# An attention and token-MLP kernel: a table of scheduler rules by stretches of 16 score tiles, filled where it was empty

## The chip, the cores and the metric

The kernel runs on one core of a Trainium2 chip. The metric is the device time of one execution in microseconds, as the median of several runs. The engines have these names in the profile: PE is TensorE (matmuls; PEld its weight loads), ACT is ScalarE, DVE is VectorE, POOL is GpSimd, SP is SyncE, which issues the DMAs.

## What is computed

The input x has 2048 rows of 640. It is normalised by row, goes once through an attention block with 32 heads of 20 columns, and once through an MLP that mixes along the rows (the "token MLP"); the result is x plus their product.

```python
xn = _layernorm(x, axis=-1)
qkv = (xn @ wqkv).reshape(B, S, 3, H, Dh).transpose(2, 0, 3, 1, 4)   # H = 32, Dh = 20, S = 2048
scores = jnp.einsum("bhqd,bhkd->bhqk", q, k) * (Dh ** -0.5)
p = _softmax(scores, axis=-1)
o = jnp.einsum("bhqk,bhkd->bhqd", p, v)
s = o.transpose(0, 2, 1, 3).reshape(B, S, D) @ wo
...
h = _layernorm(xn, axis=-1)
u = _gelu(jnp.einsum("bsd,sf->bdf", h, w1) + b1)                      # w1: 2048 x 1536
y = jnp.einsum("bdf,fs->bds", u, w2) + b2                             # w2: 1536 x 2048
g = _silu(y.transpose(0, 2, 1))
return x + s * g
```

## The kernel before

**Tiling.** The scores are computed transposed, in tiles of 128 keys by 512 queries of one head. With 32 heads, 16 key blocks and 4 query blocks there are 2048 tiles. Heads are taken in 8 groups of four; a group and a query block make a pass of 64 tiles (32 such lots in all, the last one in two halves). Three tiles of different heads run side by side on TensorE (L1279), since a head's keys fill only 32 of its rows. Of the 8 banks of PSUM, two groups of three hold score tiles, one (bank 6) collects the output of a pass, and one (bank 7) is shared by all other work and by single tiles.

**Two ways to an exponential.** Most tiles go to ScalarE, which takes the exponential of two or three banks in one instruction (`emit_exp`, L1308) into a ring of 20 buffers `pt_sb`. The rest go to VectorE in units of four tiles, one per head of the group, with one key block: VectorE turns a score into the bits of a bf16 number by an addition and a maximum (`emit_op1`, L1319), makes three shifted copies of the four tiles at once (`emit_top`, L1357), and TensorE adds the four versions with scaled copies of V (`vs_sb`), which averages out the error of that exponential. A ScalarE tile costs one PV matmul, a VectorE tile four. Both kinds of PV run in `emit_pv` (recorded at L1376, four heads side by side). At most five key blocks of a pass can go to VectorE. At the end of a pass VectorE transposes bank 6 and divides by the row sums (`ep_steps`, L1500 to L1518).

**Everything else** is cut into jobs with requirements and a due time: layer norms, the projections of q, k and v (recorded at L648 and L691), the token MLP (`mlp_steps`, L648 too, as all matmuls in column parts are recorded there; in row parts, beside score tiles, at L656), its activations (tanh on ScalarE at L844 and L849, products on VectorE), the output projection (L965), its product with g (L980, L994, in the tail L1714 and L1730), and the residual add (L1006). Due times are counted in passes: the number of score tiles started, divided by 64.

**The order of the work** is found while the program is built: `schedule()` keeps a clock for each engine with fixed costs for each operation, asks each engine for its candidates, and emits the one that can start first. The emitted order is fixed for the chip. TensorE's candidates come from `pe_cands` (L1772). Its rules are class constants:

- SLACK (0): by how many ns other TensorE work may overrun the time at which the next score tiles must start so that ScalarE doesn't wait (`lim + self.SLACK`).
- MINJ (640): of a job that needs a change of matmul kind, at most this much of its remaining run of matmuls must fit before that time (`jfit`, L1893).
- ROOM (3): with fewer free `pt_sb` buffers than this, PV goes first.
- LATE (1.0) and JOBF (4): a job overdue by more than LATE passes, or JOBF or more free buffers, put jobs ahead of PV.
- PARTS ((2,)): in which parts the PV of a VectorE unit may be taken before its copies are all done.
- LEND (1800): the third bank of a group is lent to a VectorE tile if VectorE has less than this many ns of such work before it (`do_st`, L1995).
- DON (True): whether new VectorE units may be started (`d_claimable`, L1200).
- TOPP (38), EVP (36): VectorE's precedence of the shifted copies and of evictions of PSUM, lower first (`eng_cands`, L2049).

If no candidate fits and TensorE would pause, it may emit filler matmuls (`emit_fill`, L1393).

**The table.** Before each step of the main loop, the scheduler looks whether another 16 score tiles have been started; if so it sets the constants from row `win` of PLAN, where a digit is an index into the list of that option in OPTS. PLAN is empty, so the class constants hold throughout.

```python
    def tune(self, w):
        if w < len(self.PLAN):
            for (name, vals), i in zip(self.OPTS, self.PLAN[w]):
                setattr(self, name, vals[int(i)])
...
            if nclaim[0] >= win * self.WIN:
                self.tune(win)
                win += 1
```

Of the kernel before, what the change touches and what calls it, by code (L numbers as in the profile page):

```python
# [265 lines left out]
class _Kern:  # L266
# [19 lines left out]
    SLACK, MINJ = 0.0, 640.0  # L286
# [13 lines left out]
    JOBF = 4  # L300
# [4 lines left out]
    LATE = 1.0  # L305
# [10 lines left out]
    TOPP, EVP = 38.0, 36.0  # L316
    GROT = 1
    OPTS = (
        ("SLACK", (120.0, 40.0, 200.0, 320.0)),
        ("MINJ", (640.0, 320.0, 1000.0)),  # L320
        ("ROOM", (3, 6, 0)),
        ("DRIDE", (400.0, 150.0, 700.0)),
        ("LEND", (1800.0, 1300.0, 2400.0, 700.0, 0.0)),
        ("PARTS", ((2,), (2, 1), (3, 1), (1,), ())),
        ("LATE", (2.0, -9.0, 99.0)),
        ("DON", (True, False)),
        ("LONE", (False, True)),
        ("CONFL", (True, False)),
        ("TOPP", (38.0, 22.0)),
        ("EVP", (24.0, 36.0)),  # L330
        ("FGAP", (40.0, 150.0)),
        ("GROT", (1, 0)),
    )
    PLAN = ()
    PARTS = (2,)
    DX = (1, 2, 3)
    V1A, V1B = 1.2, 3.0
# [68 lines left out]
# [4 lines that stand above are left out]
# [1770 lines left out]
```

## Time and profile before

| | us |
|---|---|
| median of 3 runs | 756.44 (756.05 to 757.03) |
| the profiled execution | 757.3 |
| its span | 755.5 |
| ScalarE busy | 730.5 (97%) |
| VectorE busy | 720.5 (95%) |
| TensorE busy | 709.7 (94%) |
| GpSimd busy | 15.5 (2%) |
| granted TensorE clock | 1.000 |

The span runs from the first to the last instruction of the profiled execution; the 1.8 us between it and the execution's time lie around it. Busy times are shares of the span. In a row of the page's groups, the line, engine, operation and tiles are followed by the count, then the busy time in us and the mean ns of one instruction, then the engine's idle time just before such instructions and what ended most of it. In the timeline and in the chain, the first number is the start in us and the second the length.

### The profile page before, as it was taken

The numbers are of one execution on the slowest core, as the hardware profiler recorded it, in microseconds if no ns is written. First come the engines' busy times: TensorE is split into PE (matmuls) and PEld (weight loads), VectorE is DVE, ScalarE is ACT, GpSimd is POOL, SyncE is SP. The second block draws the span as 40 slices with busy tenths as digits, with TensorE's granted clock in tenths as the row PEclk, the third lists the DMA queues.
The fourth block names the chain that finished last, engine by engine and source line by source line (L and its number), as shares of the span: only waits on it lengthen the run. The fifth ranks groups of instructions, "written<-read, shape, count | busy, mean of one in ns | idle before, by whom it ended". The sixth has DMA issues, their size and how long they took to land.

```text
span 755.5 us, 23583 instructions
## 1 busy us (share of the span) xinstructions
PE 709.7 (94%) x10508; PEld 242.5 (32%) x10520; DVE 720.5 (95%) x1321; ACT 730.5 (97%) x708; POOL 15.5 (2%) x23
## 2 busy tenths in 40 slices
PE   8889999999999999999999998999999999999997
PEld 7332222232233323332232232323233332332333
DVE  8899989999998999999999999999999999999997
ACT  5899999999999999999999999999999999999994
POOL 4200000000000000000000000000000000000000
PEclk9999999999999999999999999999999999999999
DMA  9745211110121301312011104122225510041012
GB/s 234 146 113 63 63 22 37 20 37 5 40 60 20 76 6 45 85 34 46 13 31 27 30 7 119 19 51 50 60 80 88 130 39 30 2 152 47 26 35 71
DMA packets 119738, 42.66 MB, mean 56 GB/s; under 512 B 79172, under 2 KB 118468, under 8 KB 119588
## 3 DMA queue, kind: packets, MB, share of 16 engines
q1 hardware_dynamic: 119636, 41.15, 23.6%
q8 instruction: 82, 1.34, 0.8%
q14 instruction: 20, 0.16, 0.1%
HBM read 26.37 MB, written 10.22 MB: 48 GB/s over the span
## 4 chain that ended last, share of the span: by engine, by line
ACT 84%; PE 11%; DVE 3%; DMA 1%; SPq 0%; issue 0%
ACT pt_sb L1308 82%; PE ps_all L648 4%; PE ps_all L1279 4%; PE ps_all L1376 3%; ACT zt_sb L849 1%; ACT zt_sb L844 1%; DMA regA<-in_A_x_dram 1%; DVE regC L568 1%; DMA xnT_sb<-regC 0%; PE ps_all L965 0%; PE ps_all L633 0%; DVE bst_sb L530 0%; DVE bst_sb L532 0%; DVE dt_sb L1319 0%; DVE v_sb L1114 0%
## 5 line engine op out<-in xcount | busy, mean ns | idle before, releaser
L1308 ACT ACTIVATE pt_sb<-ps_all 128x1024 bf16<-128x1024 f32 (+2 forms) x683 | 711.7, 1220 | 6.1 <-PE ps_all L1279 3.8
L1319 DVE TENSOR_SCALAR dt_sb<-ps_all 128x512 uint16<-128x512 f32 x496 | 327.7, 679 | 18.8 <-PE ps_all L1279 9.7
L1279 PE MATMUL ps_all<-qk_sb 32*128 32x512 bf16 (+1 forms) x2128 | 268.6, 376 | 32.5 <-ACT pt_sb L1308 28.9
L1357 DVE TENSOR_SCALAR dt_sb<-dt_sb 128x2048 uint16<-128x2048 uint16 x372 | 239.2, 683 | 1.6
L1279 PEld LDWEIGHTS ps_all<-qk_sb 32*128 32x128 bf16 x2128 | 68.3, 91 | 289.5 <-ACT pt_sb L1308 243.8
L1376 PE MATMUL ps_all<-pt_sb,v_sb 128*21 128x512 bf16 (+1 forms) x1616 | 127.0, 374 | 2.3 <-DVE v_sb L1114 1.0
L1376 PE MATMUL ps_all<-dt_sb,vs_sb 128*21 128x512 bf16 (+1 forms) x1536 | 124.1, 375 | 0.1
L648 PE MATMUL ps_all<-regB,regA 128*32 128x128 bf16 (+1 forms) x1492 | 63.6, 299 | 0.0
L648 PE MATMUL ps_all<-regC,regA 128*32 128x128 bf16 (+1 forms) x1448 | 62.5, 296 | 0.1
L1376 PE MATMUL ps_all<-dt_sb,v_sb 128*21 128x512 bf16 (+1 forms) x512 | 49.0, 378 | 0.3 <-issue 0.3
L1376 PEld LDWEIGHTS ps_all<-pt_sb,v_sb 128*21 128x21 bf16 x1616 | 32.9, 91 | 50.9 <-issue 32.5
L648 PE MATMUL ps_all<-xnT_sb,wqk_sb 128*32 128x512 bf16 x640 | 45.6, 382 | 0.2 <-DVE qs_sb L1117 0.2
L1376 PEld LDWEIGHTS ps_all<-dt_sb,vs_sb 128*21 128x21 bf16 x1536 | 30.0, 91 | 33.1 <-issue 22.9
L648 PEld LDWEIGHTS ps_all<-regB,regA 128*32 128x32 bf16 x1492 | 26.9, 96 | 25.2 <-issue 12.9
L648 PEld LDWEIGHTS ps_all<-regC,regA 128*32 128x32 bf16 x1448 | 26.2, 96 | 24.9 <-issue 14.0
L656 PE MATMUL ps_all<-regC,regA 32*128 32x512 bf16 x88 | 33.9, 385 | 0.0
L965 PE MATMUL ps_all<-wv_sb,xnT_sb 128*128 128x128 bf16 (+1 forms) x150 | 25.4, 296 | 1.9 <-issue 1.1
L1500 DVE STREAM_TRANSPOSE tr_sb<-ps_all 128x512 f32<-128x512 f32 x31 | 21.9, 706 | 0.0
L648 PE MATMUL ps_all<-wv_sb,xnT_sb 128*32 128x480 bf16 x320 | 21.1, 369 | 0.0
L1376 PEld LDWEIGHTS ps_all<-dt_sb,v_sb 128*21 128x21 bf16 x512 | 12.5, 90 | 24.3 <-issue 21.0
L648 PEld LDWEIGHTS ps_all<-xnT_sb,wqk_sb 128*32 128x32 bf16 x640 | 13.2, 95 | 18.4 <-issue 8.1
L823 DVE TENSOR_SCALAR zt_sb<-ps_all,b2h_sb 128x512 bf16<-128x512 f32 (+1 forms) x32 | 17.2, 540 | 0.6 <-PE ps_all L648 0.6
(88 smaller groups left out, 347.5 us busy)
## 6 DMA issues: line engine op xcount, KB each, us to landing
regA<-in_B_w_dram SPq DMA_DIRECT2D x6, 1024.0 KB
regA<-in_B_w_dram SPq DMA_DIRECT2D x8, 768.0 KB
qk_sb<-qk_scratch_dram SPq DMA_DIRECT2D x56, 80.0 KB
qk_scratch_dram<-qs_sb SPq DMA_DIRECT2D x32, 128.0 KB
regA<-in_A_x_dram SPq DMA_DIRECT2D x6, 640.0 KB
ok_scratch_dram<-on_sb SPq DMA_DIRECT2D x96, 20.0 KB
out_dram<-regC SPq DMA_DIRECT2D x3, 640.0 KB
wqk_sb<-in_A_wqkv_dram SPq DMA_DIRECT2D x2, 480.0 KB
```

Of the source, the lines that this page charges most:

```text
L568: steps.append(("dve", lambda e, b=b: e.tensor_scalar(regC[:, b, :], regC[:, b, :], st_sb[:, 6, b:b + 1], None, ALU.mult), [S_("r2"), S_(f ...
L648: fns.append(lambda e, c=c, e_=e_: e.matmul(oc(c, e_), lhsT[:, c:e_], rhs, start=start, stop=stop, tile_position=(0, c)))
L656: row = lambda g: (lambda e: e.matmul(oc(0, 128), lhsT[32 * g:32 * g + 32, :], rhs[32 * g:32 * g + 32, :], start=False, stop=False, tile_p ...
L823: steps.append(("dve", lambda e, z=z, i=i, jj=jj: e.tensor_scalar(z[:, c0:c0 + n], ps(bk, n, i * n), 0.5, bias[:, jj:jj + 1], ALU.mult, AL ...
L844: steps.append(("act", lambda e: e.activation(tt_, tt_, AF.Tanh, scale=1.5957691216), [stt], [stt], f"th{j}", ac(n)))
L965: steps.append(("pe", lambda e, c=c: e.matmul(ap, oT_sb[:, c, b * 128:(b + 1) * 128], wo_ap[:, c, c0:c0 + n], start=(opens and c == 0), st ...
L1279: pr.pe(lambda e, outp=outp, lhsT=lhsT, rhs=rhs, g=g: e.matmul(outp, lhsT, rhs, start=True, stop=True, tile_position=(32 * g, 0)), reads=q ...
L1308: tk = pr.act(lambda e: e.activation(outp, inp, AF.Exp, scale=math.log(2.0) / 128.0), reads=[bank_slot[b] for b in banks[:n]], writes=[S_( ...
L1319: tk = pr.dve(lambda e: e.tensor_scalar(w, src, WOFF, 0.0, ALU.add, ALU.max), reads=[bank_slot[bk]], writes=[S_(f"dt{d['tl'][0]}_{g}")], n ...
L1357: tk = pr.dve(lambda e: e.tensor_scalar(dst, src, dk, None, ALU.add), reads=[S_(f"dt{b}_{g}") for b in inb for g in range(4)], writes=[S_( ...
L1376: pr.pe(lambda e: e.matmul(outp, lhsT, rhs, start=(k == 0), stop=last, tile_position=(0, 32 * g)), reads=reads, writes=[bank_slot[AB]], na ...
L1500: steps.append(("dve", lambda e: e.transpose(tr_sb[:, :], ps(AB)), [bank_slot[AB]], [S_("tr")], f"epT{q}", 632.0))
```

## The change

PLAN gets 128 rows of 15 digits, one for each stretch of 16 score tiles. OPTS is extended so that index 0 of each list is the value of the class constant: SLACK 0.0 and LATE 1.0 are put in front, EVP is turned round, and JOBF is added. Rows of zeros restate the constants. Twenty rows hold another digit: SLACK 120 in stretch 14; LEND 2400 in 17 and in 117 to 119; TOPP 22 in 44; PARTS (1,) in 45; ROOM 6 in 58 and 59; MINJ 1000 in 82 to 89 and in 118; MINJ 320 in 91; LATE 99 with DON False in 101; LEND 1300 in 126. A row holds for its stretch and is replaced by the next one. Work, tiles and buffers are as they were.

```diff
     OPTS = (
-        ("SLACK", (120.0, 40.0, 200.0, 320.0)),
+        ("SLACK", (0.0, 120.0, 40.0, 200.0, 320.0)),
         ("MINJ", (640.0, 320.0, 1000.0)),
         ("ROOM", (3, 6, 0)),
         ("DRIDE", (400.0, 150.0, 700.0)),
         ("LEND", (1800.0, 1300.0, 2400.0, 700.0, 0.0)),
         ("PARTS", ((2,), (2, 1), (3, 1), (1,), ())),
-        ("LATE", (2.0, -9.0, 99.0)),
+        ("LATE", (1.0, 2.0, -9.0, 99.0)),
         ("DON", (True, False)),
         ("LONE", (False, True)),
         ("CONFL", (True, False)),
         ("TOPP", (38.0, 22.0)),
-        ("EVP", (24.0, 36.0)),
+        ("EVP", (36.0, 24.0)),
         ("FGAP", (40.0, 150.0)),
         ("GROT", (1, 0)),
+        ("JOBF", (4, 0, 8)),
     )
-    PLAN = ()
+    PLAN = (
...
+        "000000000000000", "000000000000000", "100000000000000", "000000000000000", "000000000000000", "000020000000000",
...
+        "000000000000000", "000000000000000", "000000000010000", "000003000000000", "000000000000000", "000000000000000",
...
+        "000000000000000", "000000000000000", "000000000000000", "000000000000000", "001000000000000", "001000000000000",
...
+        "000000000000000", "000000000000000", "000000000000000", "000000000000000", "020000000000000", "020000000000000",
+        "020000000000000", "020000000000000", "020000000000000", "020000000000000", "020000000000000", "020000000000000",
+        "000000000000000", "010000000000000", "000000000000000", "000000000000000", "000000000000000", "000000000000000",
+        "000000000000000", "000000000000000", "000000000000000", "000000000000000", "000000000000000", "000000310000000",
...
+        "000000000000000", "000000000000000", "000000000000000", "000020000000000", "020020000000000", "000020000000000",
...
+        "000010000000000", "000000000000000",
+    )
```

## The prediction

> **What bounds the kernel now.** I read the page's busy times first, then its groups of instructions, then ScalarE's idle time by stretches, then its single gaps in the timeline, and last the chain of work that ended last.
>
> ```profile
> PE 709.7 (94%) x10508; PEld 242.5 (32%) x10520; DVE 720.5 (95%) x1321; ACT 730.5 (97%) x708; POOL 15.5 (2%) x23
> ...
> ACT 84%; PE 11%; DVE 3%; DMA 1%; SPq 0%; issue 0%
> ...
> L1308 ACT ACTIVATE pt_sb<-ps_all 128x1024 bf16<-128x1024 f32 (+2 forms) x683 | 711.7, 1220 | 6.1 <-PE ps_all L1279 3.8
> L1319 DVE TENSOR_SCALAR dt_sb<-ps_all 128x512 uint16<-128x512 f32 x496 | 327.7, 679 | 18.8 <-PE ps_all L1279 9.7
> ...
> L1357 DVE TENSOR_SCALAR dt_sb<-dt_sb 128x2048 uint16<-128x2048 uint16 x372 | 239.2, 683 | 1.6
> ```
>
> Three engines are nearly full, but the chain is ScalarE's exponentials (84%). The two DVE rows are the other half of the same work: 496 of the 2048 score tiles skip ScalarE and go through VectorE, in units of four tiles (124 units; 3 x 124 = 372 shifted copies). The busy time by stretches puts ScalarE's idle time into three parts (columns: length, busy time, clock, DMA):
>
> ```profile
> 0.00:40.00 40.00, 28.51 (x29) 1.00 0.84 196
> 40.00:744.80 704.80, 702.00 (x680) 1.00 0.21 48
> 744.80:755.50 10.70, 0.00 (x1) 1.00 0.18 63
> ```
>
> So 11.5 us are ramp, 10.7 us tail, and only 2.8 us lie between. VectorE has 680.93 busy in 40 to 745, that is 24.1 us idle. The gaps of ScalarE after 43 us that the timeline marks are two:
>
> ```profile
> 520.23 6.46 ACT L1308 ACTIVATE pt_sb<-ps_all 128x1536 bf16<-128x1536 f32 x6 [0.48 <-PE ps_all L1279]
> 593.75 6.46 ACT L1308 ACTIVATE pt_sb<-ps_all 128x1024 bf16<-128x1024 f32 x6 [1.42 <-PE ps_all L1376]
> ```
>
> Around the second, the chain shows what TensorE did meanwhile: a burst of the token MLP (L648) went ahead of the PV matmuls (L1376) that had to release exponential buffers.
>
> ```profile
> 592.41 0.38 PE ps_all L1279 x3
> 592.78 0.73 PE ps_all L648 x44
> 593.51 0.26 PE ps_all L1376 x3
> 593.77 4.18 ACT pt_sb L1308 x4
> ```
>
> **What the Trainium skill says.** "Perfetto Trace Analysis", section Identifying the Most-Contended Engine: matmul busy share does not tell how close TensorE is to its limit. The trace agrees: inside TensorE's 94% are 200 filler matmuls (L1393), and its weight loads for score tiles wait 243.8 us for ScalarE. Same page, Optimization Strategy: look for the gaps of the saturated engine and ask what ends them. That is the table above, and there is little to find: 2.8 us. "TensorE: Matmul & The Clock Gate", section HAM oscillation: idle gaps over about 3.4 us lower TensorE's clock. The granted clock is 1.000 throughout here, so the change can only lose on this side; I see no reason that it does.
>
> **The change part by part.** Every index 0 of the new option lists equals the class default now in force (SLACK 0, MINJ 640, ROOM 3, LEND 1800, LATE 1, EVP 36, JOBF 4 and so on). So 108 of the 128 rows restate what holds, and reordering the lists costs nothing. Twenty rows differ. I placed them by counting score matmuls (L1279) in the trace: stretch w begins with tile 16w. Nothing runs differently before stretch 14, that is before about 98 us; the 11.5 us of ramp idle stay. After that every order differs somewhat, since the scheduler carries its state on. No instruction is added or removed by the table itself; only how many tiles VectorE takes, how exponentials are grouped, and what waits for what.
>
> Prices. A score tile costs ScalarE 711.7/1552 = 0.459 us, so one more VectorE unit saves 4 x 0.459 = 1.83 us of the bound. It costs VectorE 4 x 327.7/496 + 3 x 239.2/372 = 2.64 + 1.93 = 4.57 us. VectorE's 24.1 us idle hide up to five units on paper; only its waits for score tiles (9.7 + 6.9 us in L1319's waits, for L1279 and L656) are the kind that an order can fill, which makes three. On TensorE a unit turns 4 PV matmuls into 16, three more groups of four; at 0.98 us for 16 matmuls (the chain's L648 row of that count), 12 cost 0.74 us, beside ScalarE's work. If that cover is gone it costs at most 0.74 us of the 1.83.
>
> - Stretch 14 (98 to 105 us, SLACK 120) and 17 (115 to 122, LEND 2400): ScalarE has no gap there. VectorE idles 1.83 us just before 101, but that gap is already open when stretch 14 begins. 14 lets TensorE overrun ScalarE's due time by 0.12 us, which is the most it can cost per group; I take 0. 17 lends a bank more readily: part of a unit.
> - 44 and 45 (267 to 278 us; VectorE's shifted copies ahead of evictions, PV in single parts), 58 and 59 (346 to 358, ROOM 6: PV earlier): ScalarE has 0 and 0.04 us idle there. Worth 0; wrong order there could cost up to a gap like the largest seen, 1.42.
> - 82 to 89 (480 to 525 us, MINJ 1000): a burst of other matmuls needs more room before ScalarE's due time. The 0.48 us gap at 520 follows a burst of 68 small MLP matmuls, 17 steps of 60 ns in the scheduler's own costs, just what the larger limit holds back. Worth 0 to 0.48. 91 (531 to 536, MINJ 320) loosens it again: 0.
> - 101 (587 to 595 us, LATE 99, DON off): LATE 99 takes away the precedence of overdue jobs over PV, DON off keeps new VectorE tiles out for 16 tiles. This is the place of the 1.42 us gap and of its cause. Worth 0 to 1.42. What DON costs: about four VectorE tiles go elsewhere; if no later stretch takes them, one unit is lost, +1.83.
> - 117 to 119 (681 to 698 us, LEND 2400, MINJ 1000 in 118): more lending. VectorE is busy 21.90 of 22.00 us there, so the tiles pulled in push out residual adds (L1006, L980), which fill the last 25 us. 126 (from 732 us, LEND 1300): less lending right before the end, so that VectorE ends with less behind it.
>
> The tail after 744.8 us runs through PV, output matmuls and VectorE:
>
> ```profile
> 746.92 0.86 PE ps_all L965 x4
> ...
> 749.13 0.60 DVE regC L1714
> 749.73 1.76 DVE regC L1006 x2
> ...
> 752.14 0.61 DVE regC L1714
> ```
>
> The two residual adds (1.76 us) stand before the last product; done earlier they would give up to 1.76 us; pushed work could add as much. Its sign isn't in the trace; I take 0 and keep -1.8 to +1.8.
>
> **Sum.** Of the two gaps' 1.90 us I take 1.2, since the order before them has moved as well. Of the units I take one: two more lending stretches than stretches that forbid, and waits worth three; bounds 0 and 2 (0 to 3.66 us). Tail 0. Together 1.2 + 1.83 = 3.0 us. The profiled execution took 757.3 us (755.5 us span and 1.8 us around it); it becomes 754.3. The median of the three runs is 756.44, 0.9 below; there the sum gives 753.4 us, -0.4%.
>
> **Rivals.** (a) More: two units and both gaps, 3.66 + 1.90 = 5.6, 750.9 us; with the residual adds out of the tail 749.1. For it: VectorE's idle time would bear it. Against: each of 32 groups of 64 tiles already has about 16 VectorE tiles, most of the 20 that it may have.
> (b) It doesn't do what it says: the rules change the order but ScalarE keeps 1552 tiles, and new small gaps eat the two old ones: -0.5, 755.9 us. For it: only 2.8 us of gaps exist, and the plan comes from the scheduler's rounded costs; an exponential is 50 ns plus tiles there, VectorE's shifted copy 597 ns against 643 measured. Against: its costs stand close enough to the trace that the whole middle idles 0.4%.
> (c) Slower: held-back TensorE work comes back where there is no room. The stricter MINJ of 480 to 525 us moves MLP matmuls (L648) later, into 587 to 610; in 588 to 596 TensorE is busy 8.00 of 8.00 us. One MLP job of 48 matmuls costs 3 x 0.98 = 2.9 us there, all on ScalarE's path, as no filler lies beside it. It decides as soon as one whole job lands there: +2.9, less the 0.5 of the earlier gap, 758.8 us. Loss of a unit to DON off would bring it to 760.7. Against: from 682 to 745 us TensorE has no MLP work at all, so lateness has room behind it, and filler stands in 610 to 682 (20 matmuls).
>
> **How the numbers follow.** About 0.2% (1.5 us) is what a measurement of this kernel tells from no change. Forecast and its neighbourhood (752.0 to 754.9): 0.47. (a) below 752.0: 0.17. (b) 754.9 to 758.0: 0.20. (c) above 758.0: 0.16. So faster 0.64, same 0.20, slower 0.16. The range 750.0 to 758.4 leaves out some 0.05 below (the tail's gain on top of (a)) and 0.13 above.
>
> **What the profile after would show.** Right: L1319 at 500 (496 if no unit is gained), L1308's busy time down by about 1.8 us, no gap over 0.4 us on ScalarE near 520 and 594, ScalarE's last exponential near 742, VectorE's waits in L1319 down, the tail still about 10.7 us. Rival (b): L1319 at 496 and ScalarE's idle in the middle again 2 to 3 us. Rival (c): a chain with L648 pieces between exponentials after 580 us and gaps there of over 2 us in sum. The forecast is wrong in kind if the time moved but L1308's count of tiles and its gaps did not: then it is the tail, or a lower TensorE clock.

## The result, and the profile after

| | before | after |
|---|---|---|
| median, us | 756.76 (6 runs) | 754.17 (6 runs, 753.87 to 754.70) |
| ratio | | 0.9967 (0.9955 to 0.9979) |
| profiled execution, us | 757.3 | 753.96 |
| its span, us | 755.5 | 752.1 |

The kernel is 2.59 us faster (0.3%); the interval of the ratio leaves out 1. The page after, with 24 more lines in the program, so L1308, L1319, L1357 are now L1332, L1343, L1381 (and L648, L656, L1006, L1279, L1376, L1714 are L672, L680, L1030, L1303, L1400, L1738):

```profile
PE 709.3 (94%) x10480; PEld 240.8 (32%) x10480; DVE 717.0 (95%) x1314; ACT 731.9 (97%) x707; POOL 15.3 (2%) x23
...
ACT 80%; PE 13%; DVE 5%; DMA 1%; SPq 0%; issue 0%; DVEq 0%
...
L1332 ACT ACTIVATE pt_sb<-ps_all 128x1024 bf16<-128x1024 f32 (+1 forms) x682 | 713.6, 1229 | 4.6 <-PE ps_all L1303 3.6
L1343 DVE TENSOR_SCALAR dt_sb<-ps_all 128x512 uint16<-128x512 f32 x492 | 327.0, 684 | 20.3 <-PE ps_all L680 10.0
```

ScalarE is busier than before, by 1.4 us, and VectorE has 492 tiles: one unit less, not one more. The execution became shorter although its longest engine got more work. To see where, I cut both spans at the same two events, the first exponential after the last small gap of ScalarE's start-up (at 42.76 us before, 41.70 after) and the end of the last exponential. The three parts are called ramp, middle and tail from here on (columns: length, ScalarE's busy time, clock, DMA). Before:

```profile
0.00:42.76 42.76, 31.09 (x32) 1.00 0.87 202
42.76:744.81 702.05, 699.42 (x677) 1.00 0.21 48
744.81:755.50 10.69, 0.00 (x0) 1.00 0.18 63
```

After:

```profile
0.00:41.70 41.70, 31.09 (x32) 1.00 0.88 207
41.70:743.65 701.95, 700.85 (x676) 1.00 0.21 47
743.65:752.10 8.45, 0.00 (x0) 1.00 0.23 80
```

The ramp is 1.06 us shorter, but it has the same order in both kernels, and in the thirteen profiles of this document its end lies between 41.70 and 43.09 us: that is a difference between executions. What the change did is in the other two rows. The middle lost 1.53 us of gaps (2.63 to 1.10 idle) and gained 1.43 us of ScalarE's work: -0.10. The tail fell by 2.24. Together -2.34, near the medians' -2.59.

The gaps of 0.48 and 1.42 us are gone; the two marked gaps that are left after the ramp are small:

```profile
541.69 11.15 ACT L1332 ACTIVATE pt_sb<-ps_all 128x1024 bf16<-128x1024 f32 x11 [0.17 <-PE ps_all L680]
612.97 8.29 ACT L1332 ACTIVATE pt_sb<-ps_all 128x1024 bf16<-128x1024 f32 x8 [0.30 <-PE ps_all L1303]
```

In the tail, the last VectorE tile tells the kernels apart. In the timelines, before

```profile
741.99 0.68 DVE L1319 TENSOR_SCALAR dt_sb<-ps_all 128x512 uint16<-128x512 f32 x1
```

and after

```profile
736.88 0.66 DVE L1343 TENSOR_SCALAR dt_sb<-ps_all 128x512 uint16<-128x512 f32 x1
```

so it starts 2.8 us and 6.8 us ahead of the end of ScalarE's last exponential. Behind it come three shifted copies, the PV matmuls of that unit, the division and the last output products. The copies end 0.3 us after the last exponential before, and 2.5 us ahead of it after.

Two pieces of about 1.1 us each make up the 2.24. The last transposition of bank 6 (L1492, after L1516) starts 1.65 us after the last exponential before and 0.54 after: 1.11 us. From the end of the divided result's transposition (L1497, after L1521) to the start of VectorE's last product (L1714, after L1738) it takes 3.65 us before and 2.56 after: 1.09 us. In that second stretch before, the two residual adds (L1006) stand on the chain that ended last, just ahead of that product; after, they run earlier, in pauses of VectorE (the first two lines), and the chain no longer has them (the others):

```profile
745.31 0.49 DVE L1030 TENSOR_TENSOR regC<-regC,regA 128x640 bf16<-128x640 bf16 x1
746.07 0.45 DVE L1030 TENSOR_TENSOR regC<-regC,regA 128x640 bf16<-128x640 bf16 x1
...
747.40 0.34 DVE regC L1754
...
747.77 1.01 DVE regC L1756
748.78 0.61 DVE regC L1738
```

That they come earlier because VectorE is done earlier with its last unit fits the timelines, but no run moves the adds alone.

### The profile page after: what moved, and what is told of

The parts are those of the page before. It is cut to its first block, busy times and chain, and to the rows that moved or that the text cites. A ratio compares the mean times of both kernels' runs of the same rounds, so it can differ in the third digit from the quotient of the medians.

```text
span 752.1 us, 23508 instructions
## 1 busy us (share of the span) xinstructions
PE 709.3 (94%) x10480; PEld 240.8 (32%) x10480; DVE 717.0 (95%) x1314; ACT 731.9 (97%) x707; POOL 15.3 (2%) x23
## 4 chain that ended last, share of the span: by engine, by line
ACT 80%; PE 13%; DVE 5%; DMA 1%; SPq 0%; issue 0%; DVEq 0%
ACT pt_sb L1332 78%; PE ps_all L1303 4%; PE ps_all L1400 4%; PE ps_all L672 3%; DVE dt_sb L1343 1%; DVE dt_sb L1381 1%; ACT zt_sb L873 1%; ACT zt_sb L868 1%; PE ps_all L989 1%; PE ps_all L657 1%; DVE regC L592 1%; DMA regA<-in_A_x_dram 1%; DMA xnT_sb<-regC 0%; PE ps_all L1417 0%; DVE bst_sb L554 0%
## 5 line engine op out<-in xcount | busy, mean ns | idle before, releaser
L1332 ACT ACTIVATE pt_sb<-ps_all 128x1024 bf16<-128x1024 f32 (+1 forms) x682 | 713.6, 1229 | 4.6 <-PE ps_all L1303 3.6
L1343 DVE TENSOR_SCALAR dt_sb<-ps_all 128x512 uint16<-128x512 f32 x492 | 327.0, 684 | 20.3 <-PE ps_all L680 10.0
L1303 PE MATMUL ps_all<-qk_sb 32*128 32x512 bf16 (+1 forms) x2128 | 267.6, 376 | 32.5 <-ACT pt_sb L1332 29.0
L1381 DVE TENSOR_SCALAR dt_sb<-dt_sb 128x2048 uint16<-128x2048 uint16 x369 | 238.4, 689 | 1.5
L1303 PEld LDWEIGHTS ps_all<-qk_sb 32*128 32x128 bf16 x2128 | 67.9, 91 | 290.3 <-ACT pt_sb L1332 242.6
L1400 PE MATMUL ps_all<-pt_sb,v_sb 128*21 128x512 bf16 (+1 forms) x1624 | 126.4, 373 | 2.2 <-DVE v_sb L1138 1.0
L1400 PE MATMUL ps_all<-dt_sb,vs_sb 128*21 128x512 bf16 (+1 forms) x1512 | 123.4, 376 | 0.4 <-DVE dt_sb L1381 0.4
L672 PE MATMUL ps_all<-regB,regA 128*32 128x128 bf16 (+1 forms) x1484 | 64.4, 298 | 0.4 <-DVE zt_sb L847 0.2
L672 PE MATMUL ps_all<-regC,regA 128*32 128x128 bf16 (+1 forms) x1448 | 62.5, 296 | 0.1
L1400 PEld LDWEIGHTS ps_all<-pt_sb,v_sb 128*21 128x21 bf16 x1624 | 32.4, 91 | 51.4 <-issue 33.0
L1400 PE MATMUL ps_all<-dt_sb,v_sb 128*21 128x512 bf16 (+1 forms) x504 | 48.6, 380 | 0.0
L672 PE MATMUL ps_all<-xnT_sb,wqk_sb 128*32 128x512 bf16 x640 | 45.0, 382 | 0.2 <-DVE qs_sb L1141 0.2
L1400 PEld LDWEIGHTS ps_all<-dt_sb,vs_sb 128*21 128x21 bf16 x1512 | 29.5, 90 | 32.2 <-issue 21.5
L672 PEld LDWEIGHTS ps_all<-regB,regA 128*32 128x32 bf16 x1484 | 27.1, 96 | 26.3 <-issue 13.6
L672 PEld LDWEIGHTS ps_all<-regC,regA 128*32 128x32 bf16 x1448 | 26.2, 96 | 25.0 <-issue 14.0
L680 PE MATMUL ps_all<-regC,regA 32*128 32x512 bf16 x88 | 33.8, 384 | 0.0
L989 PE MATMUL ps_all<-wv_sb,xnT_sb 128*128 128x512 bf16 (+1 forms) x160 | 27.0, 301 | 0.2 <-DVE regC L1004 0.2
L672 PE MATMUL ps_all<-wv_sb,xnT_sb 128*32 128x480 bf16 x320 | 21.5, 369 | 0.0
L1400 PEld LDWEIGHTS ps_all<-dt_sb,v_sb 128*21 128x21 bf16 x504 | 12.3, 90 | 24.6 <-issue 21.5
L680 PE MATMUL ps_all<-regB,regA 32*128 32x512 bf16 x52 | 20.0, 385 | 0.0
L672 PEld LDWEIGHTS ps_all<-xnT_sb,wqk_sb 128*32 128x32 bf16 x640 | 13.3, 95 | 18.2 <-issue 6.6
```

Of the source, the lines that this page charges most:

```text
L672: fns.append(lambda e, c=c, e_=e_: e.matmul(oc(c, e_), lhsT[:, c:e_], rhs, start=start, stop=stop, tile_position=(0, c)))
L680: row = lambda g: (lambda e: e.matmul(oc(0, 128), lhsT[32 * g:32 * g + 32, :], rhs[32 * g:32 * g + 32, :], start=False, stop=False, tile_p ...
L989: steps.append(("pe", lambda e, c=c: e.matmul(ap, oT_sb[:, c, b * 128:(b + 1) * 128], wo_ap[:, c, c0:c0 + n], start=(opens and c == 0), st ...
L1303: pr.pe(lambda e, outp=outp, lhsT=lhsT, rhs=rhs, g=g: e.matmul(outp, lhsT, rhs, start=True, stop=True, tile_position=(32 * g, 0)), reads=q ...
L1332: tk = pr.act(lambda e: e.activation(outp, inp, AF.Exp, scale=math.log(2.0) / 128.0), reads=[bank_slot[b] for b in banks[:n]], writes=[S_( ...
L1343: tk = pr.dve(lambda e: e.tensor_scalar(w, src, WOFF, 0.0, ALU.add, ALU.max), reads=[bank_slot[bk]], writes=[S_(f"dt{d['tl'][0]}_{g}")], n ...
```

## The experiments

From here on **theory 1** says that the end is set by what VectorE and TensorE still have to do after ScalarE's last exponential, and above all by when the last VectorE unit comes; **theory 2**, that of the prediction, that time follows ScalarE's busy time and gaps. All kernels are variants of the changed one, so their line numbers are the same. A difference, in us, is of medians, a negative one being faster, against the kernel before as it ran on the same chip.

**The table up to stretch 101** (e1). Rows 117 to 119 and 126 are set to zeros.

```diff
-        "000000000000000", "000000000000000", "000000000000000", "000020000000000", "020020000000000", "000020000000000",
+        "000000000000000", "000000000000000", "000000000000000", "000000000000000", "000000000000000", "000000000000000",
...
-        "000010000000000", "000000000000000",
+        "000000000000000", "000000000000000",
```

> Only the rows up to stretch 101 of the table are kept; 117 to 119 and 126 are zeros. Theory 1 (the end is set by what VectorE and TensorE still have to do after ScalarE's last exponential): VectorE keeps 496 tiles, the two gaps of ScalarE close, its last exponential ends about 2 us earlier than before, but the tail after it grows by 1 to 1.5 us; total -0.5 to -1.3 us against before, so less than half of the full table's -2.6. Theory 2 (time follows ScalarE's busy time and gaps): the gaps' 1.4 us and no lost unit, total -1.4 to -2.0 with a tail as before, 10.7 us.

Measured 756.14 against 756.88: -0.74 (ratio 0.9988, 0.9980 to 0.9996).

```profile
42.11:742.41 700.30, 699.21 (x677) 1.00 0.21 48
742.41:754.30 11.89, 0.00 (x1) 0.94 0.16 57
```

The middle is 1.75 us shorter than before, the tail 1.20 longer: two thirds of what closing the gaps gives ScalarE is lost again at the end. The last VectorE tile, counted from the end of the ramp, comes only 0.6 us earlier. This is as theory 1 has it.

**One digit alone** (e2): row 91, MINJ 320, all others zeros. Against a table of zeros it differs in the line of rows 90 to 95 alone:

```diff
-        "000000000000000", "000000000000000", "000000000000000", "000000000000000", "000000000000000", "000000000000000",
+        "000000000000000", "010000000000000", "000000000000000", "000000000000000", "000000000000000", "000000000000000",
```

> One digit alone: stretch 91 with MINJ 320, all else zeros. Theory 1: in the order that follows, the last VectorE unit of the last half pass has three of its four tiles started only after ScalarE's last exponential, so the tail holds its four tiles' way through VectorE, PV and the output projection: tail of 17 to 19 us instead of 10.7, time +6 to +8 us against before. Theory 2: VectorE keeps 496 tiles and ScalarE's last exponential is 0.5 to 1 us earlier, so time -0.5 to -1.

Measured 764.07: +7.19 (1.0090, 1.0076 to 1.0103). ScalarE's middle even became shorter by 1 us, the tail is 18.84:

```profile
42.18:743.26 701.08, 699.45 (x676) 1.00 0.21 48
743.26:762.10 18.84, 0.01 (x1) 0.74 0.10 36
```

In VectorE's timeline, three tiles of the last unit come more than 5 us after the last exponential. They go one at a time: VectorE waits 0.48 us for the score matmuls of the second and of the third, and TensorE had waited 0.79 us before each of these matmuls for VectorE's tile ahead:

```profile
748.72 0.69 DVE L1343 TENSOR_SCALAR dt_sb<-ps_all 128x512 uint16<-128x512 f32 x1
749.89 0.69 DVE L1343 TENSOR_SCALAR dt_sb<-ps_all 128x512 uint16<-128x512 f32 x1 [0.48 <-PE ps_all L1303]
751.07 0.69 DVE L1343 TENSOR_SCALAR dt_sb<-ps_all 128x512 uint16<-128x512 f32 x1 [0.48 <-PE ps_all L1303]
```

This run also shows that row 91 alone closes the 1.42 us gap (no gap near 593 us is marked in it), while the 0.48 us gap near 520 stays.

**The full table without row 91** (e3).

```diff
-        "000000000000000", "010000000000000", "000000000000000", "000000000000000", "000000000000000", "000000000000000",
+        "000000000000000", "000000000000000", "000000000000000", "000000000000000", "000000000000000", "000000000000000",
```

> The full table without the digit of stretch 91. Theory 1: again the last VectorE unit is left over behind the last exponential (one of its tiles is started after it): tail of about 16 us, time +5 to +7 us against before, so +8 to +9 against the full table. Theory 2: VectorE has 492 tiles as in the full table and ScalarE's sum is 1 us higher, so about -1.5 against before.

Measured 762.70: +5.82 (1.0076, 1.0062 to 1.0089), tail 15.90, the last VectorE tile 5.9 us after the last exponential. As theory 1 has it. The same digit that does harm alone is needed in the full table.

**The last four digits alone** (e4): rows 117 to 119 and 126, the rest zeros. Against a table of zeros:

```diff
-        "000000000000000", "000000000000000", "000000000000000", "000000000000000", "000000000000000", "000000000000000",
+        "000000000000000", "000000000000000", "000000000000000", "000020000000000", "020020000000000", "000020000000000",
...
-        "000000000000000", "000000000000000",
+        "000010000000000", "000000000000000",
```

> Only the rows 117 to 119 and 126; the earlier ones are zeros. If those rows shorten the tail by themselves: -1 to -2.5 us against before. If they do so only in the order that the earlier rows leave (theory 1 in its strong form, the result hangs on how the last units fall): VectorE keeps 496 tiles and none is saved from the tail; ScalarE's last exponential is later by 1 to 1.5 us, time +1.5 to +3 us.

Measured 758.34: +1.46 (1.0023, 1.0014 to 1.0033), just below the +1.5 of the strong form. The middle grew by 1.59 us, the tail stayed (10.53). So what these rows do depends on the order they meet.

**One VectorE unit more** (e5): row 104, LEND 700, alone. Against a table of zeros:

```diff
-        "000000000000000", "000000000000000", "000000000000000", "000000000000000", "000000000000000", "000000000000000",
+        "000000000000000", "000000000000000", "000030000000000", "000000000000000", "000000000000000", "000000000000000",
```

> One digit alone: stretch 104 with LEND 700, all else zeros. In the order that follows VectorE takes 500 tiles, one unit more than before, which is what the prediction counted on. Theory 2 (ScalarE's sum sets the time): ScalarE's last exponential ends 2.5 to 3 us earlier and the time is 754 to 755. Theory 1 (the end is set by what is left after it): the last VectorE unit has a tile that is started some 15 us after the last exponential, the tail is about 25 us and the time +11 to +13 us against before, 768 to 770.

Measured 770.04 against 756.82: +13.22 (1.0166, 1.0152 to 1.0181), just above theory 1's range, with a unit more, as the prediction had counted on (the row lends less, where the prediction looked to rows that lend more):

```profile
41.75:743.17 701.42, 697.80 (x677) 1.00 0.21 47
743.17:768.70 25.53, 0.00 (x0) 0.87 0.15 52
```

ScalarE has 1.62 us less to do in the middle and the kernel is 13 us slower: the last tile of VectorE starts 14.5 us after the last exponential. ScalarE's end is only 0.6 us earlier rather than 2.5 to 3, since it idles 3.6 us, 1.0 more than before; the rest is theory 1. The unit more and its lateness come together here: a unit more with the last one early was not run.

**Taking the late unit away** (e6 to e8). The last half pass may have one VectorE unit in place of two:

```diff
-                dunits.append([(6, (0, 1)), (7, (2, 3))])
+                dunits.append([(6, (0, 1)), (7, (2, 3))][:2 - HALF[q]])
```

e6 does this to e2:

> The table of the run with the digit of stretch 91 alone (+7.2 us), and the very last half pass may have only one VectorE unit in place of two; its four tiles go to ScalarE. Theory 1: the unit that was left over behind the last exponential is what cost the time; without it the tail falls from 18.8 to about 9.5 us and ScalarE gains four tiles (+1.8 us), so -0.3 to -0.8 us against before, some 8 us less than with the unit. Theory 2: ScalarE's four more tiles make it 1.8 us slower than with the unit, +9.

Measured 755.32: -1.50 (0.9974, 0.9964 to 0.9984), 8.7 us less than with the unit.

```profile
42.31:745.17 702.86, 701.24 (x677) 1.00 0.21 47
745.17:753.90 8.73, 0.00 (x1) 1.00 0.22 77
```

The tail is 10.1 us shorter than in e2, ScalarE's work in the middle 1.79 us more. This shows that the late unit cost the time; the gain is larger than theory 1 expected.

e7 does it to e1:

> The table up to stretch 101 (which alone gave -0.7), with zeros from there on, and one VectorE unit in the last half pass in place of two. Theory 1: what the rows 117 to 126 bring is one late VectorE unit less in the tail, so this brings the same: tail 9 to 9.5 us, 492 tiles, -1.9 to -2.7 us against before, within 0.5 us of the full table. Theory 2, or if the rows 117 to 126 do something else: four more tiles for ScalarE, so slower than the table up to 101 by 1.8, about +1 against before.

Measured 754.65: -2.17 (0.9965, 0.9953 to 0.9977). The full table's ratio was 0.9967: without a digit after stretch 101, one late unit less gives the same, within the intervals.

e8 does it with a table of zeros:

> The table all zeros, and one VectorE unit in the last half pass in place of two: the tail's part of the gain alone, without the closing of the two gaps. Theory 1: tail 10.7 to about 9 us, ScalarE +1.3 to +1.8 us, so +0.2 to -0.6 us against before: neither part alone brings the gain, since closing the gaps moves ScalarE and the shorter tail lets the end follow. If the tail alone were the cause: -2.

Measured 755.66: -1.16 (0.9986, 0.9979 to 0.9992), between theory 1's range and the -2 of the tail alone: the tail fell to 7.79, not 9. So the expectation that neither part alone brings the gain was wrong: the rows that close the gaps gave 0.74, the late unit's removal 1.16, both together 2.17.

```profile
42.24:746.01 703.77, 701.14 (x677) 1.00 0.21 47
746.01:753.80 7.79, 0.00 (x0) 1.00 0.24 84
```

**A control: a unit less elsewhere** (e9). Zeros in the table, and pass 8 may have three units.

```diff
-                dunits.append([(c, (r,)) for r, c in enumerate(RC)])
+                dunits.append([(c, (r,)) for r, c in enumerate(RC)][:3 if q == 8 else 5])
```

> A control: the table all zeros, and one pass in the first third of the run (pass 8) may have three VectorE units in place of five. VectorE then has 492 tiles, as with the full table, but the last two half passes keep two units each. If fewer VectorE units as such bring the gain: -1 to -2.5 us against before. Theory 1 (a unit costs because it is late): ScalarE's four more tiles are paid (+1.8) and the tail is not shorter, so +1.5 to +3.5 us.

Measured 760.59 against 756.65: +3.94 (1.0048, 1.0034 to 1.0062), a little above theory 1's range.

```profile
42.68:746.61 703.93, 701.02 (x675) 1.00 0.21 47
746.61:758.80 12.19, 0.01 (x1) 0.96 0.16 55
```

VectorE has 492 tiles as in the full table, the middle is 1.88 us longer than before and the tail 1.50. Not fewer units, but one less at the end, is what helps. The control is not a pure one: in its order the last VectorE tile also comes later, 1.1 us ahead of the last exponential's end. And it closes both of the prediction's gaps, near 520 and 594, with a table of zeros (a new one of 1.08 us stands at 687.75).

**Searching on** (e10, e11). e10 is the full table after a longer search, with 51 rows that differ from zeros; e11 a table with 31 such rows for the kernel of e8. The edits are in the table's rows alone, and for e11 in the line shown for e6 to e8.

> The full table after a longer search of the same kind, 51 rows with another digit, 492 tiles as in the full table; by the scheduler's own costs it ends 1.2 us sooner than the full table, with ScalarE's last exponential 1.2 us sooner. If what the scheduler gains comes through on the chip as it did for the full table (-2.6 measured for -3.2): -3 to -4.2 us against before, -0.5 to -1.5 against the full table. If such small gains are lost in what its costs leave out: within 0.8 us of the full table.

> A table found in the same way for the kernel that may have only one VectorE unit in the last half pass, 31 rows with another digit, 492 tiles; by the scheduler's own costs 1.3 us sooner than the full table. Theory 1: a tail of 8 to 9 us with ScalarE's last exponential as early as in the full table, -3 to -4.5 us against before. If the tail can't be kept short together with closed gaps: about -2, as the table up to 101 with one unit.

Measured 753.63 (-3.02; 0.9962, 0.9950 to 0.9975) and 753.83 (-2.82; 0.9960, 0.9947 to 0.9972). e10 lies at the edge of the first of its alternatives and inside the second; e11 falls 0.2 us short of theory 1's range. Both beat the kernel before; neither can be told from the full table (0.9967).

All runs beside each other, from the profiles. The fourth column is the start of the last VectorE tile, counted from the end of ScalarE's last exponential:

| kernel | VectorE tiles | middle, us | last VectorE tile, us | tail, us | median against before, us |
|---|---|---|---|---|---|
| e5 one unit more | 500 | 701.42 | +14.5 | 25.53 | +13.22 |
| e2 row 91 alone | 496 | 701.08 | +7.8 | 18.84 | +7.19 |
| e3 without row 91 | 492 | 702.61 | +5.9 | 15.90 | +5.82 |
| e9 unit less in pass 8 | 492 | 703.93 | -1.1 | 12.19 | +3.94 |
| e1 up to 101 | 496 | 700.30 | -1.7 | 11.89 | -0.74 |
| before | 496 | 702.05 | -2.8 | 10.69 | 0 |
| e4 last four digits | 496 | 703.64 | -3.7 | 10.53 | +1.46 |
| e10 longer search | 492 | 701.38 | -6.7 | 8.48 | -3.02 |
| after | 492 | 701.95 | -6.8 | 8.45 | -2.59 |
| e6 row 91, last unit out | 492 | 702.86 | -7.9 | 8.73 | -1.50 |
| e7 up to 101, last unit out | 492 | 702.04 | -9.8 | 8.68 | -2.17 |
| e11 search, last unit out | 492 | 702.76 | -10.3 | 7.50 | -2.82 |
| e8 last unit out | 492 | 703.77 | -11.4 | 7.79 | -1.16 |

Middle and tail together, taken against those of before, give each difference of medians to within 0.35 us, but for e9 (3.38 for 3.94) and e5 (14.21 for 13.22). The middle alone shows no order down the whole table; the tail does. In the last six rows, where the tail is short in all, the middle decides again: the shortest has the best median, and the two longest have the smallest gains; e11 is out of line, with the shortest tail. There theory 2 holds. In the first seven rows, from the last VectorE tile to the end it takes 10.0 (e3) to 14.2 us (e4), the fourth column and the tail taken together; where that tile is more than 6 us ahead of the last exponential's end, the tail stays at 7.5 to 8.7 us, which I take for the last exponential's own way out (not tested).

## Why the prediction held, and which of its steps did not

The forecast was -3.0 us, composed of 1.2 for gaps, 1.83 for one more unit and 0 for the tail. What came is 1.53, -1.43 and 2.24. One term was near. The other two missed by 3.26 us one way and by 2.24 the other, and so nearly cancelled: that the sum came out close is luck. Of the signs that it named for being right only one came, no gap over 0.4 us near 520 and 594. L1343 has 492 tiles, neither 500 nor 496, ScalarE's exponentials take 1.9 us more instead of 1.8 less, the last ends at 743.64 rather than 742, VectorE's waits at these tiles rose from 18.8 to 20.3 us, and the tail fell.

**The gaps: right in size, half wrong in place.** The prediction took 1.2 of 1.90 us; the middle's idle time fell by 1.53. It gave the 1.42 us gap to row 101 (LATE 99, DON off). e2 closes that gap with row 91 alone and row 101 at zero, and e9 closes both gaps with no row at all. The gap sat where one order let a burst of MLP matmuls and a pass's end meet; another order ahead of it is enough. And the worth of a closed gap was taken as its length. e1 shows 1.75 us from ScalarE's middle and 1.20 given back in the tail; between e8 and e7 it is 1.73 and 0.89. VectorE and TensorE are nearly as full as ScalarE, so their remaining work doesn't end as much earlier as ScalarE's: in e1 the last VectorE tile came 0.6 us earlier, where the last exponential came 1.75 earlier.

**The units: wrong sign.** "Of the units I take one" rested on VectorE's waits and on two more lending stretches than forbidding ones. VectorE took one unit fewer. The number of units doesn't follow from the direction of a rule: rows that lend more stand in the changed table with a unit less, and in e5 a row that lends less brought a unit more. Its price was nearly right: four tiles more raised ScalarE's busy time by 1.43 us in the middle (1.72 in e8, 1.79 in e6) where 1.83 was worked out. But e5 shows that a unit more is no gain in itself: ScalarE saved 1.62 us and the kernel lost 13.22. (The 21.90 of 22.00 us that the prediction read for rows 117 to 119 are of 681 to 703; in their own 17 us it is 16.90, which says the same.)

**The tail: the term that made the result, set at nothing.** "Its sign isn't in the trace; I take 0 and keep -1.8 to +1.8." It was -2.24, outside those bounds. The prediction named the two residual adds as what could move, for up to 1.76 us, and they did: they left the chain, in the stretch that became 1.09 us shorter. It did not name the last VectorE unit, which by the timelines lies in the other 1.11 us, and which e6 to e8 show to be a cause by itself. The timeline of before did show it: a VectorE tile 2.8 us before the last exponential's end, with its copies running until 745 us.

**The rivals.** (a), more units, did not come about. e5, with a unit more, is slower, but because its last unit is late; e9, with a unit less in pass 8, is slower too. Whether more units with an early last one would be faster was not run. (b) held in one point, that ScalarE's middle is as long as before, but not in its cause: the gaps closed and the work grew. (c) expected held-back MLP matmuls to open gaps on ScalarE from 587 us on; after, the largest there is 0.30 us, behind score tiles, and no run has MLP matmuls in its tail. A way in which such tables do become slower, a VectorE unit left over behind the last exponential, is worth +5.8 to +13.2 us and was not among the rivals. One digit can make it (e2, e5), and one digit less (e3); these digits were chosen with their orders known, so how often it happens is not shown.

**What held.** The ramp kept its order: VectorE's first instruction that differs is at 103.5 us of before's span, ScalarE's at 113.7, and stretch 14 begins at 98. The granted clock was 1.000, and no engine but those three was near full (GpSimd 2%).

**What stays open.** Which of the 20 digits are idle was not taken apart further: e1, e4 and e7 separate only the rows up to 101 from the rest. e6 and e8 came out 0.6 to 0.7 us better than the expectations' nearest values, e9 0.4 worse. Why the longer search brings so little of what its own costs promised was not tried.

## What to carry to other kernels

When three engines are busy for 94% or more, cut the span into ramp, middle and tail at events, not at round times, and ask of each engine when its last piece starts, not only how busy it is: the one whose last piece has the longest way out sets the end. Price a closed gap on the fullest engine at less than its length when others are nearly as full; here a third to a half of it arrived, by the profiles. An order found by search hangs on how the last units fall, so a single rule that looks harmless in its place (one digit at 70% of the run) can cost more than the whole search gained; keep the last work items off the slower path by rule, as e6 to e8 do in one line.

## What the runs showed of the hardware that I had not expected

In e2 and e5, two of the three kernels with a VectorE unit left over, TensorE worked at half clock in part of the tail. In e2, stretches of the tail (after the length: busy time with counts of PE, PEld, DVE, ACT and POOL, then the granted clock and DMA):

```profile
748.00:752.00 4.00, 1.64 (x9) 0.44 (x8) 2.96 (x6) 0.00 (x0) 0.00 (x0) 1.00 0.23 82
752.00:756.00 4.00, 2.97 (x43) 1.51 (x41) 2.58 (x6) 0.00 (x0) 0.00 (x0) 0.56 0.00 0
756.00:762.10 6.10, 0.85 (x3) 0.39 (x4) 2.94 (x7) 0.00 (x0) 1.15 (x1) 0.50 0.15 54
```

Sixteen PV matmuls of 256 columns then take

```profile
753.92 1.05 PE L1400 MATMUL ps_all<-dt_sb,vs_sb 128*21 128x256 bf16 x16
```

against 0.63 us for the same group in the tail of before. "TensorE: Matmul & The Clock Gate" of the Trainium skill, section HAM oscillation, speaks of idle gaps over about 3.4 us; here the clock fell after four microseconds in which TensorE was busy 41%, with no pause longer than 0.79 us since the last exponential. In e3, on the other hand, it stayed full through pauses of 0.86 and 1.88 us until 759.4, after TensorE's last matmul. What decides between the two is not shown. The half clock is a part of e2's 7.19 us only: TensorE was busy for 3.82 us at about half clock, so I estimate at most some 1.9 us. And e3's 5.82 us came without it.

In e11's profile it happened in the middle of the run. From 449.9 to 453.3 us the clock is at half, and ScalarE's largest gap follows, behind an MLP matmul:

```profile
449.90:453.30 3.40, 3.06 (x28) 0.84 (x28) 1.66 (x4) 2.54 (x3) 0.00 (x0) 0.50 0.25 43
453.59 3.28 ACT L1332 ACTIVATE pt_sb<-ps_all 128x1024 bf16<-128x1024 f32 x3 [1.15 <-PE ps_all L680]
```

TensorE's longest pause in the 4 us ahead of it is 1.35 us. Two of e11's five executions have a mean clock of 0.996 or 0.997 and the other three 0.999, so this doesn't account for its median.

In before's tail one of the residual adds took 1.44 us, while an add on GpSimd ran (749.81, 1.33 us long); the median of the six from 728 us on is 0.48. In after it is the add of 256 columns (L1756) that runs beside GpSimd's and takes 1.01 us, against 0.29 in before. That the two engines slow each other down is suggested by this, not tested.

The ramp, with the same order in each kernel, ended between 41.70 and 43.09 us in thirteen profiled executions, a spread of 1.4 us, half as large as the effect that was looked for. Spans of single profiles can't be compared at this size unless the ramp is cut off.
